# A shorter second path, the test of the softmax sums in two parts, and a new order of the second stage

## The chip, the cores and the metric

The kernel runs on one core of a Trainium2 chip. A core has five engines, each with its own instruction stream: TensorE (PE in the profile, its weight loads PEld), VectorE (DVE), ScalarE (ACT), GpSimd (POOL) and SyncE (SP). The metric is the device time of one execution in microseconds. A second number, the span, runs from the first to the last instruction that the profiler records in one execution.

## The reference

A residual sum of an attention block and a gated MLP, on 2048 tokens of width 512, in bfloat16:

```python
x = A_x                                   # [1, 2048, 512]
xn = layernorm(x)
# A: 32 heads of width 16; each query sees itself and the 255 keys before it
scores = q @ k.T * 16 ** -0.5 ; scores = where(mask, scores, -1e9)
o = softmax(scores) @ v ;  A = o.reshape(S, 512) @ wo
# B: gated MLP that mixes over the tokens
z = gelu(xn @ w_in) ; z1, z2 = z[:, :688], layernorm(z[:, 688:])
g = w_sp @ z2 + b_sp[:, None] ;  B = (z1 * g) @ w_out
out = x + A + B
```

## The kernel before

The tokens lie in 16 blocks of 128 (index t). **The first stage** normalises x, turns it, computes z and most of q, k and v. **The second stage** does the rest: token mixing, attention and the output. It has no loop of its own. Its order is the string ORDER (L60), which the loop at L779 plays step by step, so that PE's instructions, and the other engines' instructions that each step brings, stand in exactly that order in their streams:

- `S` (do_scores, L561): one burst of score matmuls for a pair (J, g), that is, 256 queries and 8 heads. There are 16 pairs with 5 bursts each (the first two with 3), 76 in all. PE works here in tiles of 32 x 64. A burst fills two of the three PSUM tiles named S, and two exponentials on ACT (L585) empty them into E.
- `m` (do_mask, L591): one multiplication on DVE that zeroes masked entries of E, 48 in all.
- `p` (pv, L505): probabilities times values for one pair, in tiles of 64 x 32, again into an S tile; then DVE turns the result by 32 x 32 blocks into ot (L531).
- `n` (normalize, L536): on DVE a reciprocal of the softmax sums into r_all (L539), two multiplications (L545), and a transpose into oT (L553).
- `g`k or a bare number: k matmuls of 128 x 128 of the unit that is open. A g unit (g_work, L435) is 16 matmuls of token mixing over half of the columns; DVE forms u (L448) from it, and after a block's second half SP issues the DMA transpose of u to uT (L455) and the load of a later wspT (L423). An f unit (f_work, L471) is 10 matmuls: 6 of uT with w_out (L478) and 4 of oT with wo (L485). At its start SP issues the load of xo, the rows of x, for block t + 2 (L463). At its end DVE adds xo (L490) and a DMA writes the block out (L496). The last block's f unit is cut into two halves of 256 columns. q units (four) finish v.

The g, f and q units share two PSUM banks (ps_x, two buffers): a unit starts only when DVE has read the unit before the last one.

**The guard.** The softmax is computed without subtracting a maximum. check_sums (L606) tests that every reciprocal in r_all lies between 2^-60 and 2^40: a comparison, a second comparison multiplied in, and a minimum along each partition, all over [128, 512]. It is called once, in the f unit of block 13 (L493), between the addition of xo and the output DMA. A small DMA (L617) lays the 128 minima into one partition (row); after the whole of ORDER, DVE takes their minimum (L800) and makes a flag (L803). All five engines load the flag (L806) and branch on it (L812). If it is set, the second path attention_with_maximum (L621) computes the attention and the outputs again, with the maximum; with these inputs it isn't set, and every engine jumps over that code to the block behind it, where L812 and L837 collect all engines at SP and end the program.

**Queues.** SP issues nearly all DMAs of the second stage in program order: a transfer whose wait isn't over holds back all that stand behind it on SP. ACT issues the last output (c0 > 0).

Of the kernel before, what the change touches and what calls it, by code (L numbers as in the profile page):

```python
# [8 lines left out]
P = 128  # L9
BF = mybir.dt.bfloat16  # L10
F32 = mybir.dt.float32
ACT = mybir.ActivationFunctionType
ALU = mybir.AluOpType
# [4 lines left out]
DH = 16  # L18
VW = DH + 1
# [6 lines left out]
NB = S_TOK // P  # L26
# [5 lines left out]
R_LOW = 2.0 ** -60  # L32
R_HIGH = 2.0 ** 40
# [24 lines left out]
MASKS = [(192, 128), (640, 256), (1088, 128)]  # L58

ORDER = """  # L60
S q4 q4 q4 q1 S 3 g4 m 1 S m 1 m 7 S 3 g6 S 4 m 6 S g4 m p S 8 S 3 m 1 g7 p S 6 m 2 S 1 g9 S 2 n
5 g3 S 5 n 4 m 1 S 3 f5 S 5 g1 m S 7 p S 7 m 1 S g1 m 9 S 6 f3 S 2 n 4 S 1 g6 m 6 S p 4 g2 S 4 n
6 S m 4 g4 S 2 m 1 m 6 m 2 S 1 g9 S 6 p S 1 m f5 S 1 m 4 f4 S n p 2 n 2 S 2 f4 S 2 m 4 g1 S 5 m
5 S 5 g4 S 1 m 5 p S 6 m g3 S 10 S 3 g6 S 2 m 3 m 4 S 1 f7 m S 3 g1 p S 8 S 7 g3 S 2 n 9 S 2 g2
m 4 S 8 m 2 g4 n S p 2 m 4 S 3 m 3 f2 S 6 S 2 g2 m 6 m 1 S 7 g1 S 2 m 5 p S n 8 S g11 S 1 n m 4
m f2 S 7 S m 1 f6 p S 4 g4 S 1 m n 11 g4 S p 1 m 5 S 6 f2 S 1 n 2 m 4 S 1 g7 m 1 S 8 f1 S 5 p S
4 m g6 S 10 S g2 m 6 m 6 S 2 g4 m 3 S 6 p S 3 g4 m 2 S 9 m 1 f1 S 5 n 2 S 2 n g9 m S 7 g2 p S 7
n 1 m 1 S 2 m 3 f10 p n f10 f10 f10 f10
"""


@with_exitstack
def kernel(
# [12 lines left out]
    nc = tc.nc  # L86
# [71 lines left out]
    with ExitStack() as actx:  # L158
# [41 lines left out]
        for _ in range(WARM):  # L200
# [7 lines left out]
            out=hmask[:],  # L208
# [190 lines left out]
    def late():  # L399
        if not late_pool:  # L400
            assert not work["q"]
            pq_ctx.close()
            late_pool.append(
                late_ctx.enter_context(tc.tile_pool(name="late", bufs=1, side="right"))
            )
        return late_pool[0]
# [64 lines left out]
    def f_work(t, c0):  # L471
        if c0 == 0 and t + 2 < NB:
            load_xo(t + 2)
        xo = xos[t]
        w = f_cols(t)
        fo = ps_x.tile([P, 512], F32, name="fo", tag="f")
        for ch in range(NFC):
            nc.tensor.matmul(  # L478
                fo[:, 0:w], lhsT=uTs[t][:, ch, :], rhs=w_out_sb[:, ch, c0 : c0 + w],
                start=(ch == 0), stop=False,  # L480
            )
            yield
        q0 = t % 2 * P
        for c in range(NC):
            nc.tensor.matmul(  # L485
                fo[:, 0:w], lhsT=oTs[t // 2][:, c, q0 : q0 + P], rhs=wo_sb[:, c, c0 : c0 + w],
                start=False, stop=(c == NC - 1),
            )
            yield
        nc.vector.tensor_tensor(  # L490
            out=xo[:, c0 : c0 + w], in0=fo[:, 0:w], in1=xo[:, c0 : c0 + w], op=ALU.add
        )
        if t == NB - 3:  # L493
            check_sums()
        eng = nc.scalar if c0 > 0 else nc.sync
        eng.dma_start(out=out2[t * P : (t + 1) * P, c0 : c0 + w], in_=xo[:, c0 : c0 + w])  # L496

# [2 lines left out]
    later = []  # L500
# [35 lines left out]
    def normalize(J, g):  # L536
        ot = turned.pop((J, g))
        rsum = r_all[:, 2 * J + g, :]
        nc.vector.reciprocal(  # L539
            out=rsum, in_=ot[:, :, :, DH].rearrange("p h b -> p (h b)")  # L540
        )
        on = late().tile([P, 2, 8, 32], BF, name="on", bufs=2)
        for h in range(2):
            r = rsum[:, 16 * h : 16 * h + 16].rearrange("p (e b) -> p e b", e=2)
            nc.vector.tensor_tensor(  # L545
                out=on[:, h].rearrange("p b (e d) -> p e b d", e=2),
                in0=ot[:, h].rearrange("p (e b) j -> p e b j", e=2)[:, :, :, 0:DH],
                in1=r.unsqueeze(3).to_broadcast([P, 2, 8, DH]),
                op=ALU.mult,
            )  # L550
        if g == 0:
            oTs[J] = late().tile([P, NC, 256], BF, name="oT", bufs=3)
        nc.vector.transpose(  # L553
            out=oTs[J][:, 2 * g : 2 * g + 2, :].rearrange("p h q -> p (h q)"),
            in_=on[:].rearrange("p h b j -> p (h b j)"),
        )

    pairs = [(J, g) for J in range(NJ) for g in range(2)]
    groups = [(J, g, i) for J, g in pairs for i in range(len(bursts(J)))]
# [43 lines left out]
                v = v.rearrange("p x (u q) -> p x u q", q=P)  # L603
        nc.vector.tensor_tensor(out=v, in0=v, in1=mask, op=ALU.mult)  # L604

    def check_sums():  # L606
        assert not (later or units)
        r = r_all[:].rearrange("p a b -> p (a b)")
        ok = late().tile([P, 512], BF, name="ok")
        low = late().tile([P, 1], F32, name="least")  # L610
        nc.vector.tensor_scalar(out=ok[:], in0=r, scalar1=R_LOW, scalar2=None, op0=ALU.is_ge)
        nc.vector.scalar_tensor_tensor(
            out=ok[:], in0=r, scalar=R_HIGH, in1=ok[:], op0=ALU.is_le, op1=ALU.mult
        )
        nc.vector.tensor_reduce(out=low[:], in_=ok[:], axis=mybir.AxisListType.X, op=ALU.min)
        row = late().tile([P, P], F32, name="row")
        nc.sync.dma_start(out=row[0:1, :], in_=low[:])  # L617
        rows.append(row)


    def attention_with_maximum(gctx):  # L621
        X = mybir.AxisListType.X
# [32 lines left out]
        with tc.For_i(0, NG, 1) as G:  # L655
# [12 lines left out]
            with tc.For_i(0, NB, 1) as t:  # L668
                work = gen.tile([P, 4, NK], F32, name="work", bufs=2)
                keep, minus, sc = work[:, 0, :], work[:, 1, :], work[:, 2, :]  # L670
                nc.vector.tensor_tensor(
                    out=keep, in0=band[:], in1=valid[:, bass.ds(t * P, NK)], op=ALU.mult
                )
                nc.vector.tensor_scalar(
                    out=minus, in0=keep, scalar1=1.0, scalar2=NEG,
                    op0=ALU.subtract, op1=ALU.mult,
                )
                nc.vector.tensor_scalar(
                    out=keep, in0=keep, scalar1=SM_SCALE, scalar2=None, op0=ALU.mult
                )  # L680
                win = wspp.tile([P, NB * P], BF, name="win", tag="wspT")
                kw, qw = win[:, 0:NK], win[:, NK : NK + KW]
                vw = win[:, NK + KW : NK + KW + 3 * VG].rearrange("p (k w) -> p k w", k=3)
                nc.vector.tensor_copy(out=kw, in_=kx[:, bass.ds(t * P, NK)])
                nc.vector.tensor_copy(
                    out=qw.rearrange("p (e q) -> p e q", e=2), in_=qx[:, :, bass.ds(t * P, P)]
                )
                nc.vector.tensor_copy(out=vw, in_=vx[:, bass.ds(t, 3), :])
                for hh in range(8):
                    s, e = divmod(hh, 2)  # L690
                    sp = ps_x.tile([P, NK], F32, name="sp", tag="f")
                    nc.tensor.matmul(
                        sp[:], lhsT=qw[32 * s : 32 * s + 32, e * P : e * P + P],
                        rhs=kw[32 * s : 32 * s + 32, :],
                        start=True, stop=True,
                    )
                    nc.vector.tensor_tensor(out=sc, in0=sp[:], in1=keep, op=ALU.mult)
                    nc.vector.tensor_tensor(out=sc, in0=sc, in1=minus, op=ALU.add)
                    top = sm.tile([P, 1], F32, name="top")
                    nc.vector.tensor_reduce(out=top[:], in_=sc, axis=X, op=ALU.max)  # L700
                    nc.vector.tensor_scalar(
                        out=top[:], in0=top[:], scalar1=-1.0, scalar2=None, op0=ALU.mult
                    )
                    p = cp.tile([P, NK], BF, name="p", tag="u")
                    nc.scalar.activation(
                        out=p[:], in_=sc, func=ACT.Exp, bias=top[:], scale=1.0
                    )
                    pT = cp.tile([P, 3, P], BF, name="pT", tag="uT", bufs=4)
                    turn(pT, p, 3)
                    op = ps_x.tile([P, VW], F32, name="op", tag="f")  # L710
                    for k in range(3):
                        nc.tensor.matmul(
                            op[:], lhsT=pT[:, k, :],
                            rhs=vw[:, k, hh * VW : hh * VW + VW],
                            start=(k == 0), stop=(k == 2),
                        )
                    rs = sm.tile([P, 1], F32, name="rs1")
                    nc.vector.reciprocal(out=rs[:], in_=op[:, DH : DH + 1])
                    nc.vector.tensor_scalar(
                        out=oa[:, bass.ds(t, 1), bass.ds(G * P + hh * DH, DH)].rearrange(  # L720
                            "p o d -> p (o d)"),
                        in0=op[:, 0:DH], scalar1=rs[:], scalar2=None, op0=ALU.mult,
                    )

        with tc.For_i(0, NB, 1) as t:
            row0 = t * P
# [115 lines left out]
```

## Time and profile before

| | |
|---|---|
| median of 3 runs (lowest to highest) | 261.59 us (261.41 to 261.72) |
| profiled execution | 262.08 us |
| its span | 260.3 us |
| mean granted TensorE clock | 0.995 |
| second stage | from 84.4 us to the end |

The profile is of one execution. A row of a group of instructions tells line, engine, operation, tiles and shapes, count, then busy time, mean duration in ns, and the idle time just before with what ended it. The waits view has: who waited for whom, total us, times, longest us. The chain of waits is followed back from the last instruction: start, us, engine and line. The view of one source line has one row for each engine and operation with shortest, median and longest duration in ns, and the first and the last start in us. A "q" behind an engine's name means its sequencer, which issues instructions, branches and waits on semaphores.

### The profile page before, as it was taken

Reading aid. Unit: us, or ns where it says so; the run is one execution under the profiler, and the core shown is the slowest. Engines: PE = TensorE matmul, PEld = TensorE weight load, DVE = VectorE, ACT = ScalarE, POOL = GpSimd, SP = SyncE. Lnnn points to the kernel's source line nnn. Section 1 sums busy time; section 2 is a strip of 40 time slices with the busy share of each in tenths; the row PEclk is TensorE's granted clock in tenths of the full one; section 3 lists DMA queues with packets and bytes.
Section 4 is the critical chain, followed back from the end, with each engine's and each line's share of the span. In section 5 each row is a group of like instructions: output and inputs, shape, how many; then the busy total and the mean of one; then the engine's idle time right before and its main releaser. Section 6 shows DMA issues by size and latency. Waiting matters only on the chain.

```text
span 260.3 us, 9101 instructions
## 1 busy us (share of the span) xinstructions
PE 250.2 (96%) x4053; PEld 137.2 (53%) x4053; DVE 177.9 (68%) x367; ACT 190.7 (73%) x228; POOL 16.5 (6%) x52
## 2 busy tenths in 40 slices
PE   7899999999999999999999999999999999999980
PEld 2565555555555455454655455555555645555550
DVE  4795997875456756846668945478596774568881
ACT  2677546546546988989898889898987797987500
POOL 4120311211011000000000000000000000000000
PEclk9999999999999999999999999999999999999997
DMA  6994031026201215663753627623839367334332
GB/s 203 373 230 168 0 62 21 0 54 137 54 0 43 65 18 97 144 152 25 165 94 70 169 57 113 161 59 83 155 65 146 62 147 111 74 85 76 22 72 69
DMA packets 65788, 25.40 MB, mean 98 GB/s; under 512 B 53664, under 2 KB 65232, under 8 KB 65744
## 3 DMA queue, kind: packets, MB, share of 16 engines
q1 hardware_dynamic: 64256, 23.74, 43.4%
q10 hardware_dynamic: 1488, 1.03, 1.3%
q8 instruction: 33, 0.54, 0.9%
q14 instruction: 11, 0.09, 0.1%
HBM read 8.41 MB, written 2.10 MB: 40 GB/s over the span
## 4 chain that ended last, share of the span: by engine, by line
PE 89%; DMA 4%; DVE 3%; SPq 1%; ACTq 1%; issue 0%; DVEq 0%
PE gf L442 30%; PE zp L291 13%; PE S L576 10%; PE S L524 7%; PE fo L478 7%; PE pj_o L128 6%; PE pj_f L128 5%; PE fo L485 5%; DMA w_in_sb<-in_B_w_in_dram 3%; PE pj_f L146 3%; PE pj_o L146 3%; DMA xo<-in_A_x_dram 1%; DVE E L604 1%; SPq L463 1%; PE tp L281 1%; DVE ot L531 0%
## 5 line engine op out<-in xcount | busy, mean ns | idle before, releaser
L585 ACT ACTIVATE E<-S 128x1024 bf16<-128x1024 f32 x152 | 141.4, 1019 | 15.8 <-PE S L576 15.4
L442 PE MATMUL gf<-z2n,wspT 128*128 128x344 bf16 x512 | 85.8, 310 | 0.0
L442 PEld LDWEIGHTS <-wspT 128*128 128x128 bf16 x512 | 45.7, 98 | 31.5 <-issue 10.6
L291 PE MATMUL zp<-w_in_sb,xnT 128*128 128x344 bf16 x256 | 41.9, 309 | 0.7 <-DMA w_in_sb<-in_B_w_in_dram 0.7
L604 DVE TENSOR_TENSOR E<-E,maskFD 128x1024 bf16<-128x1024 bf16 (+2 forms) x48 | 38.1, 810 | 4.7 <-ACT E L585 4.7
L531 DVE STREAM_TRANSPOSE ot<-S 128x1024 f32<-128x1024 f32 x16 | 20.0, 1248 | 21.1 <-PE S L524 21.1
L291 PEld LDWEIGHTS <-xnT 128*128 128x128 bf16 x256 | 24.9, 98 | 15.9 <-issue 0.9
L576 PE MATMUL S<-qpad,kT 32*64 32x512 bf16 (+3 forms) x960 | 31.9, 309 | 0.0
L448 DVE SCALAR_TENSOR_TENSOR u<-gf,b_all,z 128x344 bf16<-128x344 f32 x32 | 18.2, 567 | 17.6 <-PE gf L442 10.2
L478 PE MATMUL fo<-w_out_sb,uT 128*128 128x512 bf16 (+1 forms) x102 | 25.2, 368 | 0.8 <-DVE xo L490 0.8
L298 ACT ACTIVATE z<-zp 128x688 bf16<-128x688 f32 x16 | 11.9, 744 | 15.1 <-PE zp L291 15.1
L576 PEld LDWEIGHTS <-kT 32*64 32x64 bf16 x960 | 10.8, 102 | 22.1 <-issue 21.1
L524 PE MATMUL S<-E,v_y 64*32 64x256 bf16 (+2 forms) x960 | 21.6, 231 | 0.0
L524 PE MATMUL S<-E,vx 64*32 64x256 bf16 (+1 forms) x960 | 21.6, 232 | 0.0
L524 PEld LDWEIGHTS <-vx 64*32 64x32 bf16 x960 | 18.1, 90 | 4.2 <-issue 4.1
L298 ACT ACTIVATE z2n<-zp 128x688 bf16<-128x688 f32 x16 | 11.9, 744 | 10.9 <-PE zp L291 10.9
L524 PEld LDWEIGHTS <-v_y 64*32 64x32 bf16 x960 | 18.9, 90 | 0.7 <-issue 0.6
L128 PEld LDWEIGHTS <-wqkv 128*128 128x128 bf16 x128 | 12.5, 98 | 12.4
L128 PE MATMUL pj_o<-xnT,wqkv 128*128 128x512 bf16 x72 | 18.5, 379 | 0.0
L485 PE MATMUL fo<-wo_sb,oT 128*128 128x512 bf16 (+1 forms) x68 | 17.8, 368 | 0.0
L139 DVE TENSOR_SCALAR qpad<-qt,hmask 128x512 bf16<-128x512 bf16 x32 | 9.7, 345 | 11.8 <-ACT qt L137 11.8
L249 POOL TENSOR_TENSOR rs<-ve,mhalf 128x2 f32<-128x2 f32 (+1 forms) x17 | 11.6, 683 | 70.3 <-DVE ve L246 70.3
(57 smaller groups left out, 196.5 us busy)
## 6 DMA issues: line engine op xcount, KB each, us to landing
xo<-in_A_x_dram SPq DMA_DIRECT2D x16, 128.0 KB, 3.3
out_dram<-xo SPq DMA_DIRECT2D x15, 128.0 KB, 2.6
vx<-v_y SPq DMA_DIRECT2D x16, 102.0 KB, 2.9
xt<-in_A_x_dram SPq DMA_DIRECT2D x3, 512.0 KB, 9.3
wqkv<-in_A_wqkv_dram SPq DMA_DIRECT2D x1, 1536.0 KB, 10.6
w_in_sb<-in_B_w_in_dram ACTq DMA_DIRECT2D x2, 344.0 KB, 6.9
w_in_sb<-in_B_w_in_dram SPq DMA_DIRECT2D x2, 344.0 KB, 5.6
w_out_sb<-in_B_w_out_dram SPq DMA_DIRECT2D x1, 640.0 KB, 5.8
```

The source lines that it names most:

```text
L128: nc.tensor.matmul(pt[:], lhsT=wqkv[:, c, w0 : w0 + P], rhs=xnT[:, c, t0 : t0 + 512], start=(c == 0), stop=(c == NC - 1),)
L291: nc.tensor.matmul(zp[:, j, 0:HALF], lhsT=xnT[:, c, n * P : (n + 1) * P], rhs=w_in_sb[:, c, f0 : f0 + HALF], start=(c == 0), stop=(c == NC ...
L298: nc.scalar.activation(out=dst.rearrange("p (j f) -> p j f", j=2), in_=zp[:, :, 0:HALF], func=ACT.Gelu_apprx_tanh,)
L442: nc.tensor.matmul(gf[:, 0:HALF], lhsT=wspT[t][:, c, :], rhs=z2n[:, c, j * HALF : (j + 1) * HALF], start=(c == 0), stop=(c == NB - 1),)
L448: nc.vector.scalar_tensor_tensor(out=u[:, j * HALF : (j + 1) * HALF], in0=gf[:, 0:HALF], scalar=b_all[:, t : t + 1], in1=z1[:, t, j * HALF ...
L478: nc.tensor.matmul(fo[:, 0:w], lhsT=uTs[t][:, ch, :], rhs=w_out_sb[:, ch, c0 : c0 + w], start=(ch == 0), stop=False,)
L485: nc.tensor.matmul(fo[:, 0:w], lhsT=oTs[t // 2][:, c, q0 : q0 + P], rhs=wo_sb[:, c, c0 : c0 + w], start=False, stop=(c == NC - 1),)
L524: nc.tensor.matmul(o[32 * s : 32 * s + 32, h, q0 : q0 + ni * KB], lhsT=v, rhs=Et[part, s, e, c0 : c0 + ni * KB], start=(i == 0), stop=(i = ...
L531: nc.vector.transpose(out=ot[:].rearrange("p h b j -> p (h b j)"), in_=o[:].rearrange("p h c -> p (h c)"))
L576: nc.tensor.matmul(o.rearrange("p (e q) -> p e q", e=2)[:, :, c0 - b0 : c0 - b0 + ni * KB], lhsT=kT[32 * s : 32 * s + 32, 2 * g + h, k0 : ...
L585: nc.scalar.activation(out=Et[:, 2 * i : 2 * i + 2, :, b0 : b0 + w].rearrange("p s e q -> p (s e) q"), in_=S[i][:].rearrange("p s (e q) -> ...
L604: nc.vector.tensor_tensor(out=v, in0=v, in1=mask, op=ALU.mult)
```

## The change

1. **ORDER is laid out anew.** The same steps stand in another order: 76 S, 48 m, 16 p, 16 n, 32 g, 17 f and 4 q units. The last steps were `... S 2 m 3 f10 p n f10 f10 f10 f10` and are `... S 5 f5 m 5 p f1 n 9 f10 f10 f10`.
2. **The test of the sums has two parts.** normalize calls it: after the 15th pair for the first 15 pairs (480 columns; their minimum is kept in column 32 of the tile least), and after the 16th pair for its 32 columns alone; then one minimum over 33 columns, and the same small DMA to row. The call in f_work is gone.
3. **The second path is shorter.** P is transposed by a DMA on ACT's queue and not by PE and a copy on DVE; the minus sign is in the reduction; the 8 heads of a group gather in one PSUM tile and are divided once. `turn` stays for u and o.

Counted in the built programs (waits and register operations included), the distance from the branch at L812 to the block behind the second path is, in instructions:

| engine | PE | DVE | ACT | SP | POOL |
|---|---|---|---|---|---|
| before | 290 | 181 | 83 | 87 | 75 |
| changed | 236 | 142 | 99 | 119 | 75 |

Up to the branch, each engine has as many instructions as before, but for one more on DVE and two more on SP (both waits or tests).

```diff
@@ f_work
-        if t == NB - 3:
-            check_sums()
@@ normalize
+        n = 2 * J + g
+        if n == len(pairs) - 2:
+            check_sums(0, n + 1, False)
+        elif n == len(pairs) - 1:
+            check_sums(n, 1, True)
@@
-    def check_sums():
-        assert not (later or units)
-        r = r_all[:].rearrange("p a b -> p (a b)")
-        ok = late().tile([P, 512], BF, name="ok")
-        low = late().tile([P, 1], F32, name="least")
-        nc.vector.tensor_scalar(out=ok[:], in0=r, scalar1=R_LOW, scalar2=None, op0=ALU.is_ge)
+    least = sm.tile([P, 33], F32, name="least", bufs=1)
+
+    def check_sums(first, count, last):
+        r = r_all[:, first : first + count, :].rearrange("p a b -> p (a b)")
+        if last:
+            ok = least[:, 0:32]
+        else:
+            ok = late().tile([P, count * 32], BF, name="ok")[:]
+        nc.vector.tensor_scalar(out=ok, in0=r, scalar1=R_LOW, scalar2=None, op0=ALU.is_ge)
         nc.vector.scalar_tensor_tensor(
-            out=ok[:], in0=r, scalar=R_HIGH, in1=ok[:], op0=ALU.is_le, op1=ALU.mult
-        )
-        nc.vector.tensor_reduce(out=low[:], in_=ok[:], axis=mybir.AxisListType.X, op=ALU.min)
+            out=ok, in0=r, scalar=R_HIGH, in1=ok, op0=ALU.is_le, op1=ALU.mult
+        )
+        if not last:
+            nc.vector.tensor_reduce(
+                out=least[:, 32:33], in_=ok, axis=mybir.AxisListType.X, op=ALU.min
+            )
+            return
+        low = late().tile([P, 1], F32, name="low1")
+        nc.vector.tensor_reduce(
+            out=low[:], in_=least[:], axis=mybir.AxisListType.X, op=ALU.min
+        )
         row = late().tile([P, P], F32, name="row")
         nc.sync.dma_start(out=row[0:1, :], in_=low[:])
@@ attention_with_maximum, per group
+                op = ps_s.tile([P, 2, 512], F32, name="op", tag="S")[:, 0, 0 : 8 * VW].rearrange(
+                    "p (h w) -> p h w", w=VW)
@@ attention_with_maximum, per head
-                    nc.vector.tensor_reduce(out=top[:], in_=sc, axis=X, op=ALU.max)
-                    nc.vector.tensor_scalar(
-                        out=top[:], in0=top[:], scalar1=-1.0, scalar2=None, op0=ALU.mult
-                    )
+                    nc.vector.tensor_reduce(out=top[:], in_=sc, axis=X, op=ALU.max, negate=True)
...
-                    turn(pT, p, 3)
-                    op = ps_x.tile([P, VW], F32, name="op", tag="f")
+                    nc.scalar.dma_start_transpose(out=pT[:], in_=p[:])
...
-                    rs = sm.tile([P, 1], F32, name="rs1")
-                    nc.vector.reciprocal(out=rs[:], in_=op[:, DH : DH + 1])
-                    nc.vector.tensor_scalar(
...
+                rs = sm.tile([P, 8], F32, name="rs1")
+                nc.vector.reciprocal(out=rs[:], in_=op[:, :, DH])
+                nc.vector.tensor_tensor(
```

More of the change, by code (lines that the diff above doesn't have):

```diff
@@ L60 @@
 ORDER = """
[L61 to L68, printed above, removed]
+S q4 q4 q4 q2 S 2 g1 m 5 S m 7 S 2 m 1 g6 m S 4 m 5 S 1 g4 p S 5 m 3 n 1 S 3 g7 p S 1 n 2 m 6 S
+f6 S 3 m 1 g5 S 8 m 3 S g10 S 6 p S g1 m 7 S 5 m 3 g2 m S 10 S 4 f4 S 6 g1 S 6 p S 4 m 5 S g9 S
+m 7 g2 S 5 m 4 n 1 S 4 g6 S n 2 m 4 p S 1 m 3 f3 m S 6 n 1 f2 S p 4 S m 4 g3 S 10 S 1 m 2 g3 n 3
+S 2 m 8 S g6 p S 4 m 2 m 2 S 2 f6 S 2 m 2 g4 S 10 S 2 f7 S p 3 g1 S 1 n 7 S 1 m 4 m m 2 g3 S 10
+S 3 m g7 S 7 p S 2 g6 n S 2 m 6 m 2 S f7 S 3 g5 S m 9 S 2 g5 p S 8 S 2 m 1 g4 n 3 S m 9 S f3 m 3
+n 2 S 2 f5 p S 3 m 2 g1 S 11 m 4 S n p g6 S 2 m 7 S m 1 f6 S 4 g4 S 1 n 4 m 4 S 3 g4 m p S 11 S
+1 f7 S 3 g3 m 3 S 3 m 5 S 2 g1 n 6 p S 9 g1 S 8 m 1 S 3 m 2 m 1 n f1 p S 9 g9 m S 5 n 2 g2 S m 9
+S 5 f5 m 5 p f1 n 9 f10 f10 f10
 """
@@ L708, in attention_with_maximum @@
                     pT = cp.tile([P, 3, P], BF, name="pT", tag="uT", bufs=4)
-                    turn(pT, p, 3)
-                    op = ps_x.tile([P, VW], F32, name="op", tag="f")
+                    nc.scalar.dma_start_transpose(out=pT[:], in_=p[:])
                     for k in range(3):
                         nc.tensor.matmul(
-                            op[:], lhsT=pT[:, k, :],
+                            op[:, hh, :], lhsT=pT[:, k, :],
                             rhs=vw[:, k, hh * VW : hh * VW + VW],
@@ L716, in attention_with_maximum @@
                         )
-                    rs = sm.tile([P, 1], F32, name="rs1")
-                    nc.vector.reciprocal(out=rs[:], in_=op[:, DH : DH + 1])
-                    nc.vector.tensor_scalar(
-                        out=oa[:, bass.ds(t, 1), bass.ds(G * P + hh * DH, DH)].rearrange(
-                            "p o d -> p (o d)"),
-                        in0=op[:, 0:DH], scalar1=rs[:], scalar2=None, op0=ALU.mult,
-                    )
+                rs = sm.tile([P, 8], F32, name="rs1")
+                nc.vector.reciprocal(out=rs[:], in_=op[:, :, DH])
+                nc.vector.tensor_tensor(
+                    out=oa[:, bass.ds(t, 1), bass.ds(G * P, P)].rearrange(
+                        "p o (h d) -> p (o h) d", d=DH),
+                    in0=op[:, :, 0:DH], in1=rs[:].unsqueeze(2).to_broadcast([P, 8, DH]),
+                    op=ALU.mult,
+                )
         with tc.For_i(0, NB, 1) as t:
```

## Prediction

> **What bounds the kernel now.** I read the page first, then the waits, then the chain of waits towards the end, and then what stands behind its last piece.
>
> ```profile
> span 260.3 us, 9101 instructions
> PE 250.2 (96%) x4053; PEld 137.2 (53%) x4053; DVE 177.9 (68%) x367; ACT 190.7 (73%) x228; POOL 16.5 (6%) x52
> ```
>
> PE is busy for 96% of the span. The question is whether it waits for anything in the second stage (84.4 us on). The waits view of that stretch says:
>
> ```profile
> DVE ot L531 <- PE S L524: 21.1, 14, 3.4
> ACT E L585 <- PE S L576: 15.4, 23, 1.4
> PE fo L478 <- DVE xo L490: 0.8, 1, 0.8
> ```
>
> DVE and ACT wait for PE, by 21 and 15 us. PE itself has one wait of note, 0.8 us. So an order can give back about that and little more: the second stage is the sum of PE's work, and the change leaves each S, p, g, f and q unit as it is. In ORDER I count 77 stretches of small-tile work (S, p) between whole-array work before, and 77 after, so changes between the two modes cost the same too. Where is the 0.8? The timeline, near the end:
>
> ```profile
> 249.59 0.65 DVE L490 TENSOR_TENSOR xo<-fo,xo 128x512 bf16<-128x512 f32 x1
> 250.16 0.41 DVE L611 TENSOR_SCALAR ok<-r_all 128x512 bf16<-128x512 f32 x1
> 250.60 0.69 DVE L612 SCALAR_TENSOR_TENSOR ok<-r_all,ok 128x512 bf16<-128x512 f32 x1
> 251.33 0.69 DVE L615 TENSOR_REDUCE least<-ok 128x1 f32<-128x512 bf16 x1
> 251.94 1.01 DVE L490 TENSOR_TENSOR xo<-fo,xo 128x512 bf16<-128x512 f32 x2
> 252.67 0.81 PE L478 MATMUL fo<-w_out_sb,uT 128*128 128x256 bf16 x6 [0.81 <-DVE xo L490]
> 254.59 0.14 DVE L803 TENSOR_SCALAR flag<-low 1x1 int32<-1x1 f32 x1
> ```
>
> The three instructions of the test hold DVE from 250.16 to 252.02, the addition of block 14 starts behind them, and PE's last half unit waits for the bank that it frees. Then the flag is written at 254.73. **But the span ends at 260.3: 5.6 us after the last computation.** The views of lines 812 and 837, and SP's own waits, show what that is:
>
> ```profile
> L812 SPq EVENT_SEMAPHORE  x3: 17/17/17, 255.9 to 256.0; - x3
> L812 ACTq COMPARE_BRANCH  x1: 54/54/54, 255.4 to 255.4; - x1
> L812 PEldq COMPARE_BRANCH  x1: 3902/3902/3902, 255.4 to 255.4; - x1
> L812 DVEq COMPARE_BRANCH  x1: 72/72/72, 255.4 to 255.4; - x1
> L812 POOLq EVENT_SEMAPHORE  x1: 17/17/17, 255.5 to 255.5; - x1
> L812 ACTq EVENT_SEMAPHORE  x1: 17/17/17, 255.8 to 255.8; - x1
> L812 DVEq EVENT_SEMAPHORE  x1: 21/21/21, 258.9 to 258.9; - x1
> L812 PEldq EVENT_SEMAPHORE  x1: 51/51/51, 259.3 to 259.3; - x1
> ```
>
> ```profile
> SPq L837 <- DVEq L812: 2.5, 1, 2.5
> SPq L837 <- PEq L812: 0.5, 1, 0.5
> ```
>
> The engines branch at about 255.4. POOL goes on 0.1 us later, ACT 0.4 and SP about 0.5; DVE needs 3.5 us and PE 3.9. SP, which collects them, waits 2.5 us for DVE and 0.5 more for PE. The DMA view of 254.8 to 257.5, and of the whole run, tells why:
>
> ```profile
> q14 instruction: 3, 0.02, 3.6%
> q8 instruction: 1, 0.02, 3.5%
> ```
>
> ```profile
> q8 instruction: 33, 0.54, 0.9%
> q14 instruction: 11, 0.09, 0.1%
> ```
>
> Instructions are fetched at the branch. A q8 packet is 0.54 MB / 33 = 16.4 KB; 33 of them for PE's 2 x 4053 instructions, so about 250 instructions each (256, if one has 64 bytes). A q14 packet (the other engines) has 0.09 MB / 11 = 8.2 KB, half of that: about 128. The jump's length in instructions, counted in the built program, was 75 on POOL, 83 on ACT and 87 on SP, all quick; 181 on DVE and 290 on PE, both stalled. I read it so: an engine holds the packet that it executes and the next one; a jump beyond them waits for a fetch.
>
> **The change part by part.**
>
> *The shorter second path.* None of its instructions run (the flag isn't set), so its DMA transposes on ACT's queue, its PSUM tile and its tiles cost nothing; only its length counts. PE's jump falls from 290 to 236. That is under one packet (about 250), so the target is in the current or the next packet wherever the branch lies. SP's grows from 87 to 119 and ACT's from 83 to 99, both still under 128; POOL's stays. DVE's falls from 181 to 142, which is over 128, so it depends on where its packets begin. DVE's branch is its instruction 413 and the target was 594, which missed; a window that holds the next packet ends after 413 + 128 = 541 at least. So it ends between 541 and 594, and the new target, 556, is inside for (594 - 556)/(594 - 541) = 72% of the places. One row bears on the place, from the DMA view of 187.5 to 189:
>
> ```profile
> q14 instruction: 1, 0.01, 1.3%
> ```
>
> At that time DVE was at its 314th instruction by count. If this packet is DVE's, it was fetched as DVE entered another packet at about 314, and that packet and the next end at 314 + 256 = 570 or a little later: 556 is inside. I take both engines to resume as ACT and SP do, at about 255.9, before SP asks for them. The two waits of SP then go: 2.5 + 0.5 = 3.0, less 0.1 for the two instructions themselves: **-2.9 us**, bounds -3.0 and 0 (a jump that misses still).
>
> [...]
>
> *The test in two parts.* The end after the last p, from its rows in the chain of waits for the pair before (PV ends at 239.92):
>
> ```profile
> 238.57 1.35 PE S L524 x103
> 239.94 1.26 DVE ot L531
> 241.23 0.36 DVE r_all L539
> 241.62 0.77 DVE on L545 x2
> 242.41 0.71 DVE oT L553
> 109.56 1.08 PE fo L478 x5
> ```
>
> Call the end of the last p E. oT is ready at E + 3.2 (243.12 - 239.92). The late test has three instructions of 32 or 33 columns, which the trace doesn't show. The nearest rows are the reciprocal of 32 columns, 0.36, above, and the flag, 0.14, below: 0.4 to 1.1, I take 0.6. Then block 13's addition, 0.65, ends at E + 4.45. On PE, an f unit takes 10 x 0.216 = 2.16 us (1.08 for five): block 13 from E, block 14 from E + 2.16 (its oT matmuls begin at E + 3.5, after oT), and the first half of block 15 at E + 4.33, in the bank that block 13's addition frees: a wait of 0.15. The second half waits for block 14's addition, at about E + 5.0, before it is due at E + 5.6. So 0.8 becomes 0.15: **-0.65 us**; with 0.4 to 1.1 for the test, -0.8 to -0.15. The small DMA row goes out at E + 3.8 and is needed at about E + 7, a cover of 3.2 us; before, it had 252.1 to 254.3. In SP's queue it stands where it stood, behind the last xo load and ahead of three output DMAs.
>
> The early test, (252.02 - 250.16) x 480/512 = 1.74 us, moves to behind the 15th normalize. Queued behind it on DVE are two u, one mask of 2048 and one of 1024 columns, for which the last p waits. From the groups kept apart by shape:
>
> ```profile
> L604 DVE TENSOR_TENSOR E<-E,maskFD 128x1024 bf16<-128x1024 bf16 x30 | 20.1, 675 | 1.9 <-ACT E L585 1.9
> L448 DVE SCALAR_TENSOR_TENSOR u<-gf,b_all,z 128x344 bf16<-128x344 f32 x32 | 18.2, 567 | 17.6 <-PE gf L442 10.2 <-issue 7.3
> L604 DVE TENSOR_TENSOR E<-E,maskFD 128x2048 bf16<-128x2048 bf16 x14 | 16.9, 1210 | 1.7 <-ACT E L585 1.7
> ```
>
> ```profile
> 123.17 1.75 PE gf L442 x12
> 236.80 0.35 PE S L576 x16
> ```
>
> DVE needs 1.74 + 2 x 0.57 + 1.21 + 0.68 = 4.8. In the new order PE has 18 g matmuls (0.146 each), two bursts and one f unit from that `n` to the last `p`: 2.6 + 0.7 + 2.2 = 5.5 us. It fits, with 0.7 spare; if normalize itself (0.36 + 0.77 + 0.71, with gaps 1.9) falls inside too, it doesn't, by 1.2. Between the 15th `p` and that `n` PE has 23 g matmuls and two bursts, 4.1 us, and DVE ot, an addition and a mask, 2.6; so normalize starts early and I take no cost, bounds 0 and +1.2.
>
> *The order elsewhere.* PE had no other wait of 0.15 us, so there is little to win. What could be won is inside p, which took 1.35 in the row above and 1.50 in this one of the chain; I put it at 0.5 over all 16:
>
> ```profile
> 216.13 1.50 PE S L524 x105
> ```
>
> What could be lost is a wait of the size of the one seen, 0.8, where ACT's exponentials run close. The last burst has the same PE work behind it in both orders (5 g matmuls, 50 f matmuls or their halves, one p), so ACT's work isn't pushed to the end. SP's queue has only three pairs of xo load and output swapped with uT and wspT transfers. I take +0.1, bounds -0.5 and +0.8.
>
> **Sum**: -2.9 - 0.65 + 0.1 = -3.45 on the profiled execution, 262.08 us with a span of 260.3: 258.6. The median of the runs shown, 261.59, is 0.5 below that execution, so I give 258.1 as the time.
>
> **The rivals.**
>
> 1. *Only one engine gets inside.* For it: DVE's 142 is over 128. SP then still waits the 2.5 for DVE, and only the 0.5 for PE goes: -0.4 - 0.55, or 260.6. If it were PE, nothing would go: 261.0.
> [...]
> 3. *Slower: the exponentials fall behind in the new order.* Each burst needs two of three S tiles, and ACT empties them at a mean of
>
> ```profile
> L585 ACT ACTIVATE E<-S 128x1024 bf16<-128x1024 f32 x152 | 141.4, 1019 | 15.8 <-PE S L576 15.4
> ```
>
> 0.93 us (141.4/152), 1.86 for a burst; its idle time before is 15.8. PE has 155 us for 76 bursts, 2.04 each. Where bursts stand closer than 1.86, PE waits. Against it: mean distance and last place are as before. It decides from 3.45/76 = 0.05 us for each burst; at 0.06 on all of them it would be 4.6, and the time 258.1 + 4.6 = 262.7.
>
> **How the numbers follow.** Forecast 78%; rival 1 10%; rival 2 7%; rival 3 5%. The forecast's own range is 257.3 (order at its best) to 259.3 (the early test late by 1.2). It doesn't hold 8 in 10 by itself, since some of its 78% lies outside, so the range reaches to rival 1: 257.3 to 260.6. This kernel's runs tell a difference of about 0.2% (0.5 us) from none. Faster: the forecast, rival 1 and half of rival 2, 91%; same: the other half, 4%; slower: rival 3, 5%.
>
> **What would show it.** In the changed profile, the branch rows of PE and DVE: COMPARE_BRANCH on PE short, and both next semaphore rows within 0.6 us; SP's two waits gone; the span's end 2.7 us behind the flag, not 5.6. If DVE's next row is still 3.5 us behind its branch, rival 1 holds; if PE's, nothing is won there. PE's wait on xo at the last unit is 0.4 at most. A new PE wait on L585 or on L604 in the second stage would tell against the order.

## The result, and the profile after

| | before | changed |
|---|---|---|
| median, four runs each (lowest to highest) | 261.5 us (261.13 to 261.72) | 258.25 us (258.08 to 258.75) |
| ratio of the times | | 0.988, 95% interval 0.986 to 0.990 |
| profiled execution, its span | 262.08 us, 260.3 us | 258.24 us, 256.4 us |
| start to the first `S` | 84.72 us | 84.03 us |
| first `S` to the flag's end | 170.01 us | 169.34 us |
| flag's end to the span's end | 5.58 us | 3.05 us |

The change makes the kernel 1.2% faster. Below, "the stage" is the time from the first `S` to the flag's end, and "the tail" the time from there to the span's end. Of the 3.9 us between the two spans 2.53 lie in the tail, 0.67 in the stage and 0.69 ahead of it. The last part is in a stage that the change doesn't touch; without it the difference is 3.2, about that of the medians (3.25).

The first lines of the changed kernel's page, and its two rows of instruction fetches (packets, MB, share of the DMA engines):

```profile
span 256.4 us, 9109 instructions
...
PE 249.9 (97%) x4053; PEld 137.4 (54%) x4053; DVE 178.8 (70%) x370; ACT 190.7 (74%) x228; POOL 16.6 (6%) x52
...
q8 instruction: 32, 0.52, 0.9%
q14 instruction: 10, 0.08, 0.1%
```

PE's busy time is what it was. There is one q8 packet less than before (33) and one q14 packet less (11).

The view of line 825, which is line 812 of the kernel before (durations in ns, first and last start in us):

```profile
L825 SPq EVENT_SEMAPHORE  x8: 17/17/17, 254.5 to 255.1; - x8
L825 SPq COMPARE_BRANCH  x1: 57/57/57, 254.0 to 254.0; - x1
L825 PEldq COMPARE_BRANCH  x1: 368/368/368, 254.0 to 254.0; - x1
L825 DVEq COMPARE_BRANCH  x1: 72/72/72, 254.0 to 254.0; - x1
L825 PEldq EVENT_SEMAPHORE  x1: 51/51/51, 254.4 to 254.4; - x1
L825 DVEq EVENT_SEMAPHORE  x1: 21/21/21, 254.6 to 254.6; - x1
```

PE's branch takes 0.37 us in place of 3.90, and DVE's next instruction comes 0.6 us behind its branch in place of 3.5. The first row holds something new too: SP has eight semaphore instructions here, where it had three. SP's own waits, from 250 us to the end, in the changed kernel:

```profile
SPq L819 <- DVE flag L816: 1.1, 1, 1.1
SPq L850 <- PEq L850: 0.6, 2, 0.4
SPq L495 <- DVE xo L491: 0.5, 1, 0.5
SPq L825 <- SPq L825: 0.5, 1, 0.5
```

The waits of 2.5 us for DVE and of 0.5 for PE are gone. In the second stage, the waits view of the changed kernel no longer has a row of PE waiting for xo; DVE and ACT still wait for PE:

```profile
DVE ot L530 <- PE S L523: 16.5, 12, 2.7
ACT E L589 <- PE S L580: 15.8, 21, 1.8
```

The timeline of DVE near the end, in the changed kernel (start, duration, instruction; in brackets the idle time before it and its releaser):

```profile
240.34 0.65 DVE L623 TENSOR_REDUCE least<-ok 128x1 f32<-128x480 bf16 x1
240.91 0.57 DVE L449 SCALAR_TENSOR_TENSOR u<-gf,b_all,z 128x344 bf16<-128x344 f32 x1
241.72 1.23 DVE L608 TENSOR_TENSOR E<-E,maskFD 128x2048 bf16<-128x2048 bf16 x1 [0.24 <-ACT E L589]
...
248.98 0.14 DVE L618 TENSOR_SCALAR least<-r_all 128x32 f32<-128x32 f32 x1
249.15 0.19 DVE L619 SCALAR_TENSOR_TENSOR least<-r_all,least 128x32 f32<-128x32 f32 x1
249.38 0.19 DVE L628 TENSOR_REDUCE low<-least 128x1 f32<-128x33 f32 x1
249.48 1.50 DVE L491 TENSOR_TENSOR xo<-fo,xo 128x512 bf16<-128x512 f32 x2
```

The late test takes 249.57 - 248.98 = 0.59 us. The early test costs no one anything: the mask behind it waits 0.24 us for ACT, not for the test. The windows view gives the stage from the first `S` to the flag (time; busy time of PE, PEld, DVE, ACT and POOL with counts; clock, DMA share, GB/s), first of the changed kernel:

```profile
84.03:253.37 169.34, 168.53 (x3579) 92.12 (x3578) 118.08 (x194) 143.23 (x155) 2.91 (x20) 1.00 0.52 97
```

and of the kernel before:

```profile
84.72:254.73 170.01, 168.39 (x3579) 91.82 (x3578) 117.08 (x191) 143.36 (x155) 2.87 (x20) 1.00 0.51 97
```

PE's busy time differs by 0.14; what went is 0.8 us of its idle time (170.01 - 168.39 = 1.62, and 0.81 after).

### The profile page after: what moved, and what is told of

Read it like the earlier page. It is cut to its first block, busy times and chain, and to the rows that moved or that the text cites. A ratio compares the mean times of both kernels' runs of the same rounds, so it can differ in the third digit from the quotient of the medians.

```text
span 256.4 us, 9109 instructions
## 1 busy us (share of the span) xinstructions
PE 249.9 (97%) x4053; PEld 137.4 (54%) x4053; DVE 178.8 (70%) x370; ACT 190.7 (74%) x228; POOL 16.6 (6%) x52
## 4 chain that ended last, share of the span: by engine, by line
PE 96%; DVE 1%; DMA 1%; POOL 0%; issue 0%
PE gf L443 32%; PE zp L292 15%; PE S L580 10%; PE fo L479 9%; PE S L523 8%; PE pj_o L129 6%; PE fo L486 6%; PE pj_f L129 5%; PE pj_f L147 3%; PE pj_o L147 3%; DMA xt<-in_A_x_dram 1%; PE tp L282 1%; DVE stats L240 1%; POOL rs L250 0%; DVE xo L491 0%; DVE xn L268 0%
## 5 line engine op out<-in xcount | busy, mean ns | idle before, releaser
L589 ACT ACTIVATE E<-S 128x1024 bf16<-128x1024 f32 x152 | 141.2, 1025 | 16.1 <-PE S L580 15.8
L479 PE MATMUL fo<-w_out_sb,uT 128*128 128x512 bf16 (+1 forms) x102 | 24.4, 367 | 0.0
L523 PE MATMUL S<-E,vx 64*32 64x256 bf16 (+3 forms) x960 | 21.8, 232 | 0.0
L486 PE MATMUL fo<-wo_sb,oT 128*128 128x512 bf16 (+1 forms) x68 | 17.3, 368 | 0.0
L491 DVE TENSOR_TENSOR xo<-fo,xo 128x512 bf16<-128x512 f32 (+1 forms) x17 | 11.1, 654 | 8.4 <-PE fo L486 8.1
```

What stands on the lines that cost most here:

```text
L479: nc.tensor.matmul(fo[:, 0:w], lhsT=uTs[t][:, ch, :], rhs=w_out_sb[:, ch, c0 : c0 + w], start=(ch == 0), stop=False,)
L486: nc.tensor.matmul(fo[:, 0:w], lhsT=oTs[t // 2][:, c, q0 : q0 + P], rhs=wo_sb[:, c, c0 : c0 + w], start=False, stop=(c == NC - 1),)
L523: nc.tensor.matmul(o[32 * s : 32 * s + 32, h, q0 : q0 + ni * KB], lhsT=v, rhs=Et[part, s, e, c0 : c0 + ni * KB], start=(i == 0), stop=(i = ...
L589: nc.scalar.activation(out=Et[:, 2 * i : 2 * i + 2, :, b0 : b0 + w].rearrange("p s e q -> p (s e) q"), in_=S[i][:].rearrange("p s (e q) -> ...
```

## The experiments

My theory, an estimate from the packets and the stalls in the profile before (16.4 KB on q8 and 3.90 us on PE, 8.2 KB on q14 and 3.5 us on DVE): an engine holds the packet of instructions that it executes and the next one; a jump beyond them stalls, and the change brings PE's and DVE's jumps inside. The first rival: the stall goes for another reason (the order, the test). Each experiment ran beside the kernel before, to which its ratio is; the medians of that kernel were 261.18, 261.38 and 261.34 us in the three groups of runs. All edits are shown against the changed kernel, and `...` marks what is left out.

**The short second path alone** (the old order, the old test).

```diff
-S q4 q4 q4 q2 S 2 g1 m 5 S m 7 S 2 m 1 g6 m S 4 m 5 S 1 g4 p S 5 m 3 n 1 S 3 g7 p S 1 n 2 m 6 S
...
+n 1 m 1 S 2 m 3 f10 p n f10 f10 f10 f10
@@ f_work
+        if t == NB - 3:
+            check_sums()
...
-    def check_sums(first, count, last):
+    def check_sums():
```

> Before, with the shorter second path alone (old order, old test). The jump theory: PE's and DVE's jumps (236 and 142 instructions) land inside what is held, so from the flag to the end of the span it is 3.1 us and not 5.6; time 261.5 - 2.5 = 259.0, and the wait of 0.8 us at the last half unit stays. Rival, the length does not matter: 261.5.

258.66 us, ratio 0.990 (0.989 to 0.992). The tail behind the flag is 3.07 us and the stage 169.95, as in the kernel before. In its waits PE still stands before the last unit:

```profile
PE fo L478 <- DVE xo L490: 0.8, 1, 0.8
```

So the path carries 2.5 of the 3.25 us. (The block behind the path has grown with it; its price is in the last experiment.)

**The old second path alone** (the new order, the new test).

```diff
-                    nc.scalar.dma_start_transpose(out=pT[:], in_=p[:])
+                    turn(pT, p, 3)
...
+                    rs = sm.tile([P, 1], F32, name="rs1")
+                    nc.vector.reciprocal(out=rs[:], in_=op[:, DH : DH + 1])
...
-                rs = sm.tile([P, 8], F32, name="rs1")
-                nc.vector.reciprocal(out=rs[:], in_=op[:, :, DH])
```

> The changed kernel with the old, longer second path (new order and test in two parts stay). The jump theory: PE branches over 290 instructions again and DVE over 181, both wait for a fetch, SP waits about 3 us for them: 258.25 + 2.5 = 260.8. Rival, the gain came from the order: 258.3.

260.83 us, ratio 0.998 (0.997 to 0.999). The stage is 169.38 us, as in the changed kernel, and the tail 5.99. The fetches on its page, and the branch with what follows it:

```profile
q8 instruction: 33, 0.54, 0.9%
q14 instruction: 11, 0.09, 0.1%
```

```profile
L826 PEldq COMPARE_BRANCH  x1: 4238/4238/4238, 254.1 to 254.1; - x1
L826 DVEq COMPARE_BRANCH  x1: 72/72/72, 254.1 to 254.1; - x1
...
L826 DVEq EVENT_SEMAPHORE  x1: 21/21/21, 257.3 to 257.3; - x1
```

Code that never runs brings both stalls back, 4.24 us on PE and 3.2 on DVE (254.1 to 257.3). The first rival falls.

**The old order with the new test**, and **the new order with the old test**.

```diff
-S q4 q4 q4 q2 S 2 g1 m 5 S m 7 S 2 m 1 g6 m S 4 m 5 S 1 g4 p S 5 m 3 n 1 S 3 g7 p S 1 n 2 m 6 S
...
+n 1 m 1 S 2 m 3 f10 p n f10 f10 f10 f10
```

> The changed kernel with the old order (the short path and the test in two parts stay). If the test alone is worth the 0.65 us: 258.3. My theory is that it needs the new order: in the old one the 15th normalize, and so the early test of 1.7 us, stands on DVE just ahead of the u of block 15, whose transpose on SP holds back the loads of xo for blocks 14 and 15; these land up to 1.7 us later, and the wait moves there: 259.0 to 259.6, no better than the short path alone.

```diff
@@ f_work
+        if t == NB - 3:
+            check_sums()
...
-    def check_sums(first, count, last):
+    def check_sums():
```

> The changed kernel with the old test (one test of 512 columns after block 13's addition; the new order and the short path stay). If the order alone is worth the 0.65 us: 258.3. My theory is that the test is what holds DVE between the additions of blocks 13 and 14: the wait of about 0.8 us at the last half unit comes back, 258.25 + 0.7 = 259.0.

The old order with the new test: 259.5 us, ratio 0.994 (0.992 to 0.995), stage 170.73, the longest of all so far. Two rows of its timeline show the first loss, on DVE and on PE:

```profile
243.30 0.65 DVE L623 TENSOR_REDUCE least<-ok 128x1 f32<-128x480 bf16 x1
243.87 1.82 DVE L608 TENSOR_TENSOR E<-E,maskFD 128x2048 bf16<-128x2048 bf16 x2
```

```profile
245.13 0.19 PE L523 MATMUL S<-E,v_y 64*32 64x64 bf16 x1 [0.73 <-DVE E L608]
```

In the old order the 15th `n` comes close before the last `p`, so the early test stands ahead of the last masks and PE waits 0.73 us. The second loss is in SP's queue and behind it on DVE:

```profile
250.54 0.55 SPq L632 DMA_DIRECT2D row<-low  x1
251.19 0.54 SPq L464 DMA_DIRECT2D xo<-in_A_x_dram  x1
```

```profile
253.51 0.76 DVE L491 TENSOR_TENSOR xo<-fo,xo 128x256 bf16<-128x256 f32 x2 [1.62 <-PE fo L486]
```

The small DMA waits for the late test, and the load of the last xo stands behind it: both additions of block 15 come together, late. The row names PE as the releaser, but PE had ended block 15's first half at 252.4; the load, which starts at 251.19 and takes some 2.2 us to land (the median of this kernel's xo loads at that place), is the one that fits: 253.4. PE's second half ends at 253.47 by its own row, so the load costs only what the two additions take in place of one, some 0.3 us. The two losses together are less than the 1.4 us by which this stage is longer than the changed kernel's; the cause of the rest is open.

The new order with the old test: 258.98 us, ratio 0.991 (0.989 to 0.992), stage 170.03; the old wait is back:

```profile
PE fo L479 <- DVE xo L491: 0.7, 1, 0.7
```

Neither edit alone makes the kernel faster than the short path does; with both it is 0.6 us faster by the ratios. The intervals of those two ratios overlap (0.986 to 0.990 and 0.989 to 0.992), so the stage has to carry this: it is 169.95 us with the old order and test, 169.34 in the changed kernel, and 169.27 to 169.65 in seven of the eight further kernels below and above that keep the new order, the new test and the flag's place. The eighth (170.02) is the first of the next experiment.

**Where PE's border lies.** Matmuls that never run are put into the second path of the changed kernel, 16 and then 22 of them. PE's jump is 268 and 280 instructions, not 236.

```diff
+    cold = ps_x.tile([P, 512], F32, name="cold", tag="f")
+    for _ in range(16):
+        nc.tensor.matmul(cold[:, 0:P], lhsT=ident[:], rhs=ident[:], start=True, stop=True)
     with tc.For_i(0, NG, 1) as G:
```

> The changed kernel with 16 matmuls (32 instructions) added to the second path, which does not run. PE's jump is 268 instructions, its target instruction 8378 of PE's stream. Theory of packets: PE's packets begin at multiples of 256 less 64 by the fetches' times (7872, 8128, 8384), the target is inside the next one: no change, 258.3. Rival, the bare length counts and 256 is the limit: PE stalls, 260.8.

```diff
...
+    for _ in range(22):
...
```

> The same with 22 matmuls: jump 280, target 8390, six behind the packet's end at 8384. Theory of packets: PE's branch takes 3.9 us again, and SP waits for it: the end about 2.9 us later, 261.1. Rival, the limit is somewhere between 280 and 290 or elsewhere: 258.3.

With 16: 258.66 us, ratio 0.989 (0.987 to 0.991). With 22: 260.81, ratio 0.997 (0.996 to 0.998). The branch rows, with 16 and with 22:

```profile
L828 PEldq COMPARE_BRANCH  x1: 373/373/373, 254.9 to 254.9; - x1
```

```profile
L828 PEldq COMPARE_BRANCH  x1: 4258/4258/4258, 254.1 to 254.1; - x1
```

Six more matmuls, 12 instructions, turn 0.37 us into 4.26. How many instructions a packet has is an estimate: in the changed kernel q8 packets are fetched at 35.8, 58.0 and 80.9 us, and the windows view has 257 (129 on PE and 128 on PEld) and 256 (129 and 127) of PE's matmuls and weight loads between them. A jump of 268 is over one such packet and lands inside, which fits that PE holds the next packet beyond its own. Counted from the program's start the targets are 8378 and 8390; a border at 8384 = 32 x 256 + 192 would lie between them, if the packets begin at 192, beside which the first q8 fetch comes (at 17.3 us; the windows view has 193 of PE's matmuls and weight loads up to there, 96 and 97). That PE holds two packets is not shown by this: a limit of bare length between 268 and 280 would give the same, and PE's branch was never moved. In its profiled execution the kernel with 16 has a stage of 170.02 us: the chain of waits has PE idle for 0.30 us inside one `p`, at 112.79. The cause, and that of the rest, is open; two of its four runs are at 258.1 and 258.25.

**Where DVE's border lies.** 16 and 24 memsets that never run.

```diff
+    for _ in range(16):
+        nc.vector.memset(vx[:, 0:2, :], 0.0)
     with tc.For_i(0, NG, 1) as G:
```

> The changed kernel with 16 memsets on DVE added to the second path (one is merged into a wait: the jump is 157 instructions, the target instruction 571 of DVE's stream). Theory of packets of 128: they begin at 64, 192, 320, 448, so what is held ends at 576 and the target is inside: 258.3. Rival, the limit is a length between 142 and 157: DVE stalls, SP waits 2.5 us for it, 260.5.

```diff
+    for _ in range(24):
...
```

> The same with 24 memsets: jump 165, target 579, three behind the end at 576. Theory of packets: DVE's next row comes 3.5 us behind its branch and the end is 2.4 us later, about 260.5. Rival, the limit lies nearer to the old 181: 258.3.

260.83 us, ratio 0.998 (0.996 to 0.999), and 260.74, ratio 0.998 (0.997 to 0.999): both stall, the kernel with 16 so:

```profile
L827 DVEq COMPARE_BRANCH  x1: 72/72/72, 254.2 to 254.2; - x1
...
L827 DVEq EVENT_SEMAPHORE  x1: 21/21/21, 258.1 to 258.1; - x1
```

Its jump is 157 and its target 571. I had expected 16 to land inside (a window to 576) and 24 (579) outside; the first is a miss. The border lies between 556, which is inside, and 571.

**Length or place.** 20 small memsets that do run, at DVE's start: its jump stays 142, and branch and target move on by 20, to 434 and 576.

```diff
     nc.vector.memset(warm[:], 0.0)
+    for _ in range(20):
+        nc.vector.memset(mhalf[:], -0.5)
```

> The changed kernel with 20 memsets of 128x4 on DVE at the very start, where DVE waits for the first x. The jump is 142 as in the changed kernel, but branch and target lie 20 further on: 434 and 576. Theory of packets: the packet behind the branch's own ends at most at 571 (the run with 16 memsets missed there), so the target is outside, DVE's next row comes 3.2 to 3.9 us behind its branch: 260.6. Rival, a bare length between 142 and 157 is the limit: 258.3.

260.89 us, ratio 0.999 (0.998 to 1.001); the tail is 5.48 us:

```profile
L827 DVEq COMPARE_BRANCH  x1: 72/72/72, 254.3 to 254.3; - x1
...
L827 DVEq EVENT_SEMAPHORE  x1: 21/21/21, 258.1 to 258.1; - x1
```

The same jump of 142 stalls, 3.8 us where it took 0.6. The length alone doesn't decide; the place does. The fetches say the same: in the changed kernel one q14 packet each starts at 90.0 and at 187.8 us, and with 20 instructions more at DVE's start these come at 68.0 and 170.8, while the other q14 packets between 58 and 170 us move by 0.6 us at most. That fits that these two packets are DVE's, fetched at the same places of its program in both runs.

**A longer jump at a better place.** 24 memsets that don't run and 32 that do: a jump of 165 from 446 to 611, meant to branch from behind a packet border.

```diff
+    for _ in range(32):
+        nc.vector.memset(mhalf[:], -0.5)
...
+    for _ in range(24):
+        nc.vector.memset(vx[:, 0:2, :], 0.0)
```

> The 24 memsets in DVE's second path, which cost 2.4 us (jump 165), and 32 executed memsets of 128x4 at the start: branch at 446, target at 611. Theory of packets: DVE has just entered the next packet (it begins at 443 at most), so what is held reaches to about 698 and the longer jump lands inside: 258.3, faster than without the 32 instructions. Rival, the length counts: 260.7.

263.56 us, ratio 1.008 (1.006 to 1.010). A miss twice over. DVE still stalls, for 3.7 us (257.4 to 261.1), and the first `S` comes at 87.16 us, 3.1 later than in the changed kernel. The 20 memsets had cost 0.2 there. In this run the windows view has a granted clock of 0.79 from 8 to 16 us, where the changed kernel has 1.00, which would make some 1.7 us of the 3.1, (1 - 0.79) x 8, if PE's work set the pace there; why the clock fell, and what the rest is, stays open. As for the stall: no q14 packet is fetched between 173 us and the branch, so by this sign DVE had not entered another packet. If its packets begin at 64 + 128k, as the q14 fetches beside its 194th and 314th instruction suggest (90.4 and 188.4 us in the kernel before; an estimate), the border is at 448 and the branch stood two instructions short of it. But then what is held ahead of that border would end at 576, and the target at 571 (16 memsets) would have been inside by five. The two runs fit together only if the counts are off by some instructions, or if what is held ends a little ahead of the packet's end; no run tells which. That a long jump lands inside from the right place is therefore not shown.

**The flag ahead of the last addition.** low and flag (make_flag holds the two instructions that stood behind the loop over ORDER) are computed on DVE before block 15's second half is added.

```diff
@@ f_work
+        if c0 > 0:
+            make_flag()
         nc.vector.tensor_tensor(
...
```

> The changed kernel with the last minimum and the flag ahead of the last addition on DVE, where DVE waits for PE. If the way from the flag over the load to the branch bounds the end: 0.35 us less (the minimum and the flag, 253.02 to 253.37), 257.9. My theory by now is that the last output's landing does: SP's second semaphore instruction at L825 waits for it (254.63, 1.6 us behind the issue at 253.05), whatever the flag does: 258.25, no change.

259.92 us, ratio 0.994 (0.993 to 0.996): 1.7 us slower than the changed kernel, which neither theory had expected. The flag is ready 0.8 us earlier (252.57), but the tail is 5.82 us. The last output in the DMA issues of this kernel (KB, us to landing), and SP's waits:

```profile
out_dram<-xo ACTq DMA_DIRECT2D x1, 64.0 KB, 3.2
```

```profile
SPq L829 <- SPq L829: 3.3, 2, 2.8
```

and the same output in the changed kernel:

```profile
out_dram<-xo ACTq DMA_DIRECT2D x1, 64.0 KB, 1.6
```

The output is issued at 253.34 us, 0.3 later than in the changed kernel, lands at about 256.5 and not 254.6, and SP waits 2.8 us for it. In the changed kernel it lands just as SP comes to its semaphore (254.63). The span ends some 1.8 us behind the landing in both kernels (258.4 and 256.4). So the end is held here by the last output, and the flag that is ready 0.8 us earlier wins nothing. Why the output takes twice as long: this kernel's DMA view of 254.2 to 255.5 has the code fetches of the branch,

```profile
q14 instruction: 3, 0.02, 6.9%
q8 instruction: 1, 0.02, 5.6%
```

just when the output's packets should move. In the changed kernel all 144 of them (queue q10) start between 253.9 and 254.3, before its fetches at 255.0. Here 126 start by 254.75, and 18 trail behind, as the view of 254.75 to 256.2 shows:

```profile
q10 hardware_dynamic: 18, 0.01, 4.1%
```

That these 18 are held up by the fetches is argued from the times, not shown by a run.

**Fewer transposes in the second path.** Two DMAs of four heads each, not eight of one. It runs as never as the others.

```diff
-                    nc.scalar.dma_start_transpose(out=pT[:], in_=p[:])
...
+                    if hh % 4 < 3:
+                        continue
+                    nc.scalar.dma_start_transpose(
+                        out=pT4[:], in_=p4[:].rearrange("p h k -> p (h k)"))
...
```

> The changed kernel with two transposing DMAs of four heads in the second path instead of eight of one head. It uses fewer DMA queues, so the block behind it has 5 semaphore instructions on SP instead of 8 (each 0.066 us). Theory: from the flag to the end 2.85 us instead of 3.05, the time 0.2 lower at 258.05. Rival: SP waits for something else in that time and nothing changes, 3.05.

257.79 us, ratio 0.987 (0.985 to 0.989), the lowest median of all. The tail is 2.81 us, and SP has five semaphore instructions at its branch, not eight:

```profile
L830 SPq EVENT_SEMAPHORE  x5: 17/17/17, 255.0 to 255.4; - x5
```

Its interval overlaps that of the changed kernel, so that it is the faster one is likely and not shown; the tail's 0.24 us and the three instructions are in the trace.

## Why the prediction was right, point by point

258.1 us was predicted and 258.25 measured; on the profiled execution the sum said -3.45, and -3.2 came without the start's 0.69.

- **"A jump beyond them waits for a fetch"**: right, but for DVE with 16 memsets and with the jump from 446, which were expected inside and stalled. The old path alone brings the stall back (4.24 us on PE, 3.2 on DVE), and so do never executed matmuls on PE alone (4.26 with 22) and memsets on DVE alone (3.9 with 16). The count of q8 packets is its mark: 33 in the three kernels in which PE stalls (before, the old path, 22 matmuls), 32 in the other eleven. For DVE "about 128" instructions to a q14 packet was my estimate, half of the 250 of a q8 packet as 8.2 KB is half of 16.4; no run counts them. (The 64 bytes of an instruction are an estimate too: 16.4 KB over the 257 and 256 counted between q8 fetches.) What the runs show of its window is that 142 instructions from 414 land inside (0.6 us) and 157 don't (3.9 us). That the wait is for a fetch is argued and not shown: three q14 packets and one q8 packet come about 1 us behind the branch in both kernels (256.4 us before, 255.1 in the changed kernel, with no stall), and what the kernel before has beyond them is one packet of each near its end, at 259.5 and 260.0.
- **DVE's window "ends at 570 or a little later"**: not contradicted at 570 itself (556 inside, 571 not), but that is as near as it could be. The counts are of the built program, and the border may be off by some instructions. That the packet at 188 us is DVE's, which the prediction had as an "if", is borne out by its move with the 20 memsets. Some luck is in it that DVE landed inside: the margin was under 15 instructions, and the 20 at DVE's start lost it.
- **The tail, -2.9**: the mis-sized term; it was -2.53. The waits for DVE and PE went as forecast, and the signs by which to tell came: PE's next row 0.4 us behind its branch, DVE's 0.6. What failed is "cost nothing; only its length counts", said of the transposes in the shorter path: I took SP's way to the end as unchanged, but the block behind the second path grew. With its eight transposes SP has eight semaphore instructions at its branch, where the old path left three (254.6 to 254.7); why their number grows with the transposes, no run shows. With five instead of eight (two transposes) the tail fell by 0.24, or 0.08 each; at that price five more are 0.4 us, the whole difference.
- **The end of the order, -0.65, and the rest, +0.1**: together -0.55, and the stage gave -0.67. The small test was put at 0.6 and took 0.59. The wait of PE went to nothing and not to 0.15: PE reached block 15's first half at 250.25, and the addition that frees its bank, the first of the two in the row at 249.48 (1.50 us for both), was just done, at 250.16. The runs agree: changed against the short path alone, 0.988 against 0.990, is 0.6 us, though with intervals that overlap.
- **The 0.5 "inside p"**: within the estimate of the order, and not won. In the chain of waits of the changed kernel a p still takes

```profile
244.40 1.43 PE S L523 x112
```

- **The early test at no cost**: right for this order, and only for it. With the old order PE waits 0.73 us for a mask behind it.
- **The rivals.** Only one engine inside: it didn't happen, but its price was near. 260.6 was given for DVE stalled and 260.83 came (16 memsets); 261.0 for PE stalled and 260.81 came (22 matmuls). Rival 2, that the stall isn't about the length: refuted by the old path, with which both stalls are back. The exponentials falling behind: no sign, as ACT's waits for PE are 15.8 us where they were 15.4.
- **The first stage's 0.69**: in no step of the prediction. The first `S` comes between 83.85 and 84.27 us in every other kernel but the one with 32 memsets, so the profiled execution of the kernel before (84.72) was a late one there; the medians don't need the 0.69.

## What to carry to other kernels

The branch over code that never runs had a price here: PE's branch took 3.9 to 4.3 us with jumps of 280 and 290 instructions and 0.37 with 236 and 268, and DVE's next instruction came 3.2 to 3.9 us behind its branch with jumps of 157 and 181 and with 142 from 434, and 0.6 with 142 from 414. So read the branch rows and the first instruction behind them on each engine, and keep the body short for every engine with margin, since 20 small instructions ahead of it brought 2.4 us of the tail back here. What the skipped body uses counted too: with eight transposing DMAs in it SP had eight semaphore instructions at its branch, with two it had five, and the tail was 0.24 us shorter. Where a test guards the end, most of it can be done early, but the step that it stands in front of has to be moved with it: the test or the order alone won nothing here.

## What the runs showed of the hardware that I had not expected

- The same DVE jump of 142 instructions lands inside from 414 and stalls from 434. With a stall DVE's next instruction comes 3.2 to 3.9 us behind its branch (0.6 without), and PE's branch takes 3.9 to 4.3 us (0.37 without).
- The last 64 KB output took 3.2 us to land in place of 1.6 when PE, SP and POOL branched 0.8 us earlier, and the fetches came among its packets.
- The mean granted clock on the page, 0.995 before and 1.000 after, says nothing of the work in these two: in the windows view the stage has 1.00 in both (the rows above), and only the stretch from 255 us on, where PE multiplies no more, has 0.68 before and 0.87 after.
